# Softmax attention times a gated ReLU block: heads divided on VectorE between two 32x32 turns, and the transposes of the heads left out

## The chip, the cores and the metric

The kernel runs on one core of a Trainium2 chip. The metric is the device time of one execution in microseconds; the times given are medians of several runs. A core has five engines that run side by side, each with its own instruction queue: TensorE (PE in the profile, its weight loads PEld), VectorE (DVE), ScalarE (ACT), GpSimd (POOL) and SyncE (SP). SyncE only issues DMAs here; GpSimd issues some as well.

## The reference

```python
x = A_x                                   # 1 x 2048 x 576, fp32
xn = layernorm(x)                         # rows normalized, eps 1e-5
q, k, v = split(xn @ wqkv)                # 32 heads of 18 columns
p = softmax(q @ k.T * 18 ** -0.5)         # full, over 2048 keys
s = concat_heads(p @ v) @ wo
gate = xn @ W_gate; up = xn @ W_up        # 576 x 4608 each
g = silu((relu(gate) * up) @ W_down)
out = x + s * g
```

All products keep nearly fp32 precision: an operand is split into a high part (rounded to the fast fp32r type) and a low remainder, and three products (high x high, high x low, low x high) are summed in PSUM.

## The kernel before, in words

The work is one long stream of matmuls. A small planner in the source, `Lanes` (lines 30 to 211), keeps two lanes: the upper and the lower 64 rows of TensorE's array take different matmuls at the same time. The planner gives every part a PSUM bank out of eight, counts columns as time, keeps an estimate of when VectorE ("V") and ScalarE ("A") are free (`server`), and writes out the matmuls in the order it finds. `window` (line 169) takes a list of parts, a list of score matmuls to mix in, and inserts, which are called when a given share of the columns has been written out. A function `hold` (line 78) takes a bank for a step that uses all of the array, and `pause` advances both lanes. `keep` (line 262) pins an instruction to the program's order on its engine; what is not pinned may be moved by the scheduler that lowers the program. All matmuls and transposes are pinned, and so are some VectorE operations, but not the reductions at line 394. `load` (line 267) pins SyncE's DMAs until `in_order` is cleared at line 982.

**First stage** (lines 424 to 689). Tokens come in four groups `g` of 512. Rows are loaded (`load_rows`), their statistics taken on VectorE (`stats`, line 454), normalized on VectorE (`normalized_rows`, line 476; the first group half on ScalarE, `first_rows`), and transposed to features on TensorE (`turn`, line 499). Per group one window computes q and k (`pq`), evicted by ScalarE (high part, line 303) and VectorE (low part, line 304) into four buffers `hh` and stored to DRAM by GpSimd's queue (line 554); a second window computes v (`pv`). The steps of the next group's rows are inserts of the first window (`spread`, line 658). `spill` (line 532) stores the transposed rows to DRAM, five DMAs at once after the first window. GpSimd splits the weights (`split_pool`, line 307). Before the first useful product, `busy` (line 603) issues matmuls whose result is not used. GpSimd also clears the two value tiles `va` (lines 795 to 801), early in the program.

**Middle** (lines 966 to 1009). Two interleaved streams: the gated block runs over 144 units of 128 hidden columns (`pg`, `pu` for gate and up, `py` for down), two units to a `cycle` (line 934), and attention runs over 16 pairs of heads `u`, four cycles each. A cycle mixes in 32 score matmuls `pm` for the row maxima of the next pair, each reduced on VectorE (line 394, 128 rows to one column), and 32 score matmuls `psx`, whose exponentials ScalarE takes (line 880). After a cycle `attend` (line 896) multiplies eight key tiles with the values (`po`, 64 matmuls over four column groups of the array); the first of two sums is copied by ScalarE (line 914), the second added by VectorE (line 918). The exponentials need minus the row maximum, which rides in two extra rows of `qT`: `max_rows` (line 820) reduces, splits in high and low, transposes on TensorE (line 829, tile `tp`), copies out (line 833) and writes the rows with eight small DMAs (line 839). `finish_pair` (line 845) turns the sums `ot` (head columns x tokens) into rows with four transposes (line 862), divides by the sum of exponentials that came out as a column of the same product (lines 849 to 856), and stores rows to `od`. Both are put on the list `tasks` and run after `attend` of every second cycle (line 1008).

**End** (lines 1010 to 1118). The last two units and the last attention product are done, then `store_y` writes the last group's sums to DRAM. For each of 16 token tiles the heads are loaded as rows, turned by five transposes (`heads`, line 1050), split, and multiplied with `wo` in 28 matmuls (`pw`); `load_gate` (line 1031) loads the sums, ScalarE takes the sigmoid, GpSimd the product; VectorE multiplies (line 1111), GpSimd adds `x` (line 1115, for the last two tiles VectorE), and SyncE stores the output (line 1116). Tiles are taken in the order `horder`, the last gated group last.

Of the kernel before, what the change touches and what calls it, by code (L numbers as in the profile page):

```python
# [10 lines left out]
BF16 = mybir.dt.bfloat16  # L11
# [18 lines left out]
class Lanes:  # L30
# [4 lines left out]
    def __init__(self, banks, make, matmul, fence):  # L35
        self.make, self.matmul, self.fence = make, matmul, fence
        self.t = [0.0, 0.0]
        self.last = 0.0
        self.free = [0.0] * banks
        self.used = [False] * banks  # L40
        self.server = {"V": 0.0, "A": 0.0}
        self.main = [deque(), deque()]
        self.n = self.synced = self.fences = 0
        self.wrote = [0] * banks
        self.left = []
# [40 lines left out]
    def own(self, lane, name):  # L86
# [3 lines left out]
        return b, self.make(b, name)  # L90

# [48 lines left out]
    def part(self, p):  # L140
        by = min("AV", key=lambda e: self.server[e])
# [73 lines left out]
def kernel(  # L215
# [10 lines left out]
    nc = tc.nc  # L226
# [60 lines left out]
    od = dram.tile([S, D], F32, name="od")  # L287
# [70 lines left out]

    def strips(dst, src, u, cs, order):
# [22 lines left out]
    def maxima(u, h):  # L382
# [3 lines left out]
        def one(g, j, c):  # L386
            def fn():
# [5 lines left out]
                def reduce(ps):  # L393
                    nc.vector.tensor_reduce(mx[:, g % 2, h, j, c : c + 1], ps, axis=AX.X, op=ALU.max)  # L394
                    counts[u, g // 2] += 1
                    if counts[u, g // 2] == 4 * 4 * NQ:
                        tasks.append((max_rows, ([qTs[u, g - g % 2], qTs[u, g - g % 2 + 1]], mx)))
# [26 lines left out]
    with ExitStack() as st:  # L424
# [4 lines left out]
        def weights(name, n, outs, pl=one, first=None, **kw):  # L429
            gw = pl.tile([P, 2, KS, n], F32R, name=name, **kw)  # L430
            o = 0
            for cols in outs:
# [4 lines left out]
                if first is not None:  # L437
                    keep(nc.gpsimd.tensor_copy(hi, rg))
# [15 lines left out]
        def stats(xt, ln):  # L454
# [18 lines left out]
            ln += [xt, mv, rs]  # L473
            yield

        def normalized_rows(xt, mv, rs, xn):
            for j in range(4):
                nc.vector.tensor_scalar(
                    xn[:, j, :D], xt[:, j], mv[:, j, 0:1], rs[:, j : j + 1], op0=ALU.subtract, op1=ALU.mult
                )  # L480
                nc.vector.tensor_scalar(
                    xn[:, j, D:], xt[:, j, C4:], mv[:, j, 0:1], rs[:, j : j + 1], op0=ALU.subtract, op1=ALU.mult
                )
                if j % 2:
                    yield

        def first_rows(xt, mv, rs, xn):
            nb = one.tile([P, 4], F32, name="nb")
            nc.vector.scalar_tensor_tensor(nb, mv[:, :, 0], -1.0, rs, op0=ALU.mult, op1=ALU.mult)
            for j in range(2):  # L490
                nc.scalar.activation(
                    xn[:, 2 + j, :D], xt[:, 2 + j], AF.Identity, bias=nb[:, 2 + j : 3 + j], scale=rs[:, 2 + j : 3 + j]
                )
                nc.vector.tensor_scalar(
                    xn[:, j, :D], xt[:, j], mv[:, j, 0:1], rs[:, j : j + 1], op0=ALU.subtract, op1=ALU.mult
                )
# [35 lines left out]
        def spill(g):  # L532
            for c in range(KX):
                load(xTd[g, c], xs[g][c].rearrange("p a s -> p (a s)").bitcast(F32))
# [68 lines left out]
        def busy(xt):  # L603

            ones = one.tile([P, 512], F32R, name="ones")
            half = one.tile([P, 512], BF16, name="half")
# [3 lines left out]
            nc.gpsimd.memset(half, 1.0)  # L610
# [3 lines left out]
            ops = [(ones[:, :P], ones)] * 10 + [(xr[:, :P], xr[:, :512])] * 4  # L614
            ops += [(xr[:, :P], xr[:, 0:1].to_broadcast([P, 512]))] * 4
            ops += [(half[:, :P], half)] * 4 + [(ones[:, :P], ones)] * 4 + [(xr[:, 64:192], xr[:, 1:513])] * 4
            for l, r in ops:
                mm(ps, l, r, start=True, stop=True)
# [29 lines left out]
        def stepped(gen, at_):  # L648
            return [(w, lambda: next(gen, None)) for w in at_]

        for g in range(NQ):
# [6 lines left out]
            spread = [0.1 + 0.85 * i / 12 for i in range(12)]  # L658
# [3 lines left out]
            lanes.window(parts, None, ins)  # L662
            if g + 1 < NQ:
                spill(g)
# [22 lines left out]
            lanes.window([a + b for a, b in zip(va_, vb_)], scores)  # L687
# [57 lines left out]
    def add_up(j, n, f, side):  # L745
# [5 lines left out]
        def add(ps):  # L751
            nc.vector.tensor_tensor(ys[j][:, cs], ps[:, :HC], ys[j][:, cs], ALU.add)  # L752
# [42 lines left out]
    vas = []  # L795
    for i in range(2):
        va = two.tile([P, NT, VA + 32], F32, name=f"va{i}", bufs=1)
        nc.gpsimd.memset(va, 0.0)
        nc.gpsimd.memset(va[:, :, DH : DH + 1], 1.0)
        nc.gpsimd.memset(va[:, :, VA + DH : VA + DH + 1], 1.0)  # L800
        vas.append(va)
# [14 lines left out]
    def run_tasks(todo):  # L816
        for fn, args in todo:
            fn(*args)

    def max_rows(qs, mx):  # L820
# [3 lines left out]
        nc.vector.tensor_reduce(nm, mx, axis=AX.X, op=ALU.max, negate=True)  # L824
        nxr = nx.bitcast(F32R)
        nc.scalar.activation(nxr[:, :, :, 0], nm, AF.Copy)
        nc.vector.tensor_tensor(nxr[:, :, :, 1], nm, nx[:, :, :, 0], ALU.subtract)
        b, ps = lanes.hold("tp")
        tp(ps[0:32, 0:P], nx.rearrange("p q h a j -> p (q h a j)"), ident)
        nt_ = two.tile([32, P], F32, name="nt")  # L830

        def write(ps):
            nc.scalar.activation(nt_.bitcast(F32R), ps[0:32, 0:P], AF.Copy)
            for q, qT in enumerate(qs):
                for h in range(2):
                    for a in range(2):
                        r = h * R + KA + a
                        p0 = q * 16 + h * 8 + a * 4
                        nc.sync.dma_start(
                            qT[r : r + 1, :].rearrange("o (j t) -> o j t", t=P).bitcast(F32), nt_[p0 : p0 + 4, :]  # L840
                        )
# [303 lines left out]
```

## Time and profile before

| | |
|---|---|
| median of three runs | 2634.07 us (2632.28 to 2634.75) |
| the profiled execution, its own time | 2630.82 us |
| its span in the trace | 2629.0 us |
| granted TensorE clock, mean | 0.997 |
| TensorE busy, instructions | 2604.1 us, 25546 |
| VectorE busy, instructions | 1733.4 us, 2904 |
| ScalarE busy, instructions | 1465.8 us, 2780 |
| GpSimd busy, instructions | 1443.3 us, 1276 |

Rows of the profile give a group of instructions with its line in the source, its engine, the operation, the tiles written and read, shapes and count, then the busy time in us and the mean of one in ns, then idle time ahead of it and what ended it. A row of the chain gives start, length and the piece. A row of the windows gives the stretch, its length, then busy time and number of instructions of TensorE, its weight loads, VectorE, ScalarE and GpSimd, then the granted TensorE clock (1.00 is full), the DMA engines' busy share and GB/s. Matmul durations overlap, so the distance of starts is what passes. All times in traces are of the one profiled execution.

### The profile page before, as it was taken

How to read it: one execution, taken by the hardware profiler on the slowest of the kernel's cores; microseconds unless marked ns; L12 is line 12 of the kernel's file. 1: busy time of each engine (PE TensorE's matmuls, PEld its weight loads, DVE VectorE, ACT ScalarE, POOL GpSimd, SP SyncE). 2: the span in 40 equal slices, each digit the busy share in tenths (PEclk: the TensorE clock that was granted, in tenths of full speed). 3: DMA queues.
4: the chain of work that ended last, by engine and by line, in shares of the span. 5: the costliest groups of instructions: out<-in, count | busy, mean ns of one | idle time of the engine just before them, and what ended most of it. 6: DMA issues, size and time to landing. Idle time of an engine off the chain costs nothing.

```text
span 2629.0 us, 63025 instructions
## 1 busy us (share of the span) xinstructions
PE 2604.1 (99%) x25546; PEld 2122.5 (81%) x25546; DVE 1733.4 (66%) x2904; ACT 1465.8 (56%) x2780; POOL 1443.3 (55%) x1276
## 2 busy tenths in 40 slices
PE   7999999999999999999999999999999999999999
PEld 6999888777788887777777777788877777777789
DVE  5326557777777777777777777777777777776124
ACT  2221136666666666666666666666666666666662
POOL 5236785555555555555555555555555555555555
PEclk8999999999999999999999999999999999999999
DMA  7644332222332222222242222222232222222247
GB/s 245 211 155 143 88 102 68 76 69 72 100 95 65 75 69 73 69 69 74 73 132 69 76 66 66 73 67 75 72 109 82 67 76 71 73 66 58 58 125 236
DMA packets 293267, 243.72 MB, mean 93 GB/s; under 512 B 64496, under 2 KB 236272, under 8 KB 292976
## 3 DMA queue, kind: packets, MB, share of 16 engines
q1 hardware_dynamic: 286192, 216.08, 28.3%
q0 software_dynamic: 6784, 23.60, 2.7%
q8 instruction: 202, 3.31, 0.5%
q14 instruction: 89, 0.73, 0.1%
HBM read 193.45 MB, written 45.61 MB: 91 GB/s over the span
## 4 chain that ended last, share of the span: by engine, by line
PE 93%; DMA 2%; POOL 1%; DVE 1%; SPq 1%; ACT 1%; issue 0%; ACTq 0%; POOLq 0%; DVEq 0%
PE pg L272 23%; PE po L272 17%; PE py L272 16%; PE pu L272 10%; PE psx L272 10%; PE pm L272 9%; PE pq L272 4%; PE pv L272 2%; PE pw L272 1%; PE tp L275 1%; DMA gt<-yd 0%; DMA qd<-hh 0%; DMA out_dram<-xr 0%; DMA rd<-in_B_W_down_dram 0%; PE tps L275 0%
## 5 line engine op out<-in xcount | busy, mean ns | idle before, releaser
L394 DVE TENSOR_REDUCE mx<-pm 128x1 f32<-128x512 f32 x2048 | 1379.4, 689 | 245.1 <-PE pm L272 163.3
L880 ACT ACTIVATE p<-psx 128x512 f32<-128x512 f32 x2048 | 1181.7, 598 | 542.3 <-PE pm L272 254.4
L272 PE MATMUL pg<-x,gw 64*128 64x512 f32 x3888 | 1157.2, 392 | 3.2 <-POOL gw L309 2.3
L272 PE MATMUL pu<-x,gw 64*128 64x512 f32 x3888 | 1144.2, 392 | 0.0
L272 PE MATMUL pm<-kT,qT 54*128 54x512 f32 x2048 | 793.5, 397 | 0.0
L272 PE MATMUL psx<-qT,kT 56*128 56x512 f32 x2048 | 786.0, 394 | 0.0
L272 PEld LDWEIGHTS pg<-x,gw 64*128 64x128 f32 x3888 | 719.3, 186 | 61.3 <-POOL gw L309 3.2
L272 PEld LDWEIGHTS pu<-x,gw 64*128 64x128 f32 x3888 | 717.3, 187 | 22.9
L272 PE MATMUL py<-dw,hh 64*128 64x288 f32 x6864 | 717.2, 295 | 2.1 <-POOL dw L309 0.9
L272 PEld LDWEIGHTS py<-dw,hh 64*128 64x128 f32 x6864 | 662.0, 186 | 51.6 <-issue 31.1
L272 PE MATMUL po<-p,va 128*32 128x512 f32 x4096 | 452.7, 594 | 0.4 <-ACT p L880 0.4
L730 POOL CAST hh<-h 128x512 fp32r<-128x512 f32 x127 | 77.6, 611 | 611.6 <-DVE h L727 611.6
L757 POOL TENSOR_TENSOR y<-yt,y 128x288 f32<-128x288 f32 x268 | 215.1, 806 | 325.4 <-ACT yt L756 325.3
L272 PEld LDWEIGHTS psx<-qT,kT 56*128 56x128 f32 x2048 | 375.2, 185 | 19.9
L309 POOL TENSOR_TENSOR gw<-rg,gw 128x1152 fp32r<-128x1152 f32 x144 | 383.6, 2664 | 11.6
L272 PEld LDWEIGHTS pm<-kT,qT 54*128 54x128 f32 x2048 | 371.5, 185 | 13.3
L272 PEld LDWEIGHTS po<-p,va 128*32 128x32 f32 x4096 | 126.4, 110 | 279.0 <-issue 269.0
L309 POOL TENSOR_TENSOR dw<-rd,dw 128x576 fp32r<-128x576 f32 x144 | 205.0, 1423 | 11.5
L733 POOL TENSOR_TENSOR hh<-h,hh 128x512 fp32r<-128x512 f32 x144 | 186.3, 1294 | 36.0 <-ACT hh L732 25.7
L308 POOL CAST gw<-rg 128x1152 fp32r<-128x1152 f32 x144 | 165.3, 1148 | 23.5 <-DMA qT<-qd 9.0
L752 DVE TENSOR_TENSOR y<-py,y 128x288 f32<-128x288 f32 x268 | 120.4, 449 | 50.1 <-PE py L272 49.7
L723 ACT ACTIVATE h<-pg 128x512 f32<-128x512 f32 x144 | 85.9, 596 | 112.3 <-PE pg L272 76.9
(96 smaller groups left out, 1379.4 us busy)
## 6 DMA issues: line engine op xcount, KB each, us to landing
rd<-in_B_W_down_dram SPq DMA_DIRECT2D x144, 288.0 KB
rg<-in_B_W_gate_dram SPq DMA_DIRECT2D x144, 256.0 KB
rg<-in_B_W_up_dram SPq DMA_DIRECT2D x144, 256.0 KB
qT<-qd SPq DMA_DIRECT2D x384, 36.0 KB
kT<-kd SPq DMA_DIRECT2D x384, 36.0 KB
kd<-hh POOLq DMA_DIRECT2D x16, 512.0 KB, 5.4
qd<-hh POOLq DMA_DIRECT2D x16, 512.0 KB, 6.0
xTd<-x SPq DMA_DIRECT2D x15, 512.0 KB
```

The lines of the kernel that those rows point to most:

```text
L272: return keep(nc.tensor.matmul(*args, **kw))
L275: return keep(nc.tensor.transpose(*args))
L308: keep(nc.gpsimd.tensor_copy(hi, raw))
L309: keep(nc.gpsimd.tensor_tensor(lo, raw, hi.bitcast(F32), ALU.subtract))
L394: nc.vector.tensor_reduce(mx[:, g % 2, h, j, c : c + 1], ps, axis=AX.X, op=ALU.max)
L723: nc.scalar.activation(made[0], ps, AF.Relu)
L730: keep(nc.gpsimd.tensor_copy(hh[:, 0], h))
L733: keep(nc.gpsimd.tensor_tensor(hh[:, 1], h, hh[:, 0].bitcast(F32), ALU.subtract))
L752: nc.vector.tensor_tensor(ys[j][:, cs], ps[:, :HC], ys[j][:, cs], ALU.add)
L757: keep(nc.gpsimd.tensor_tensor(ys[j][:, cs], t, ys[j][:, cs], ALU.add))
L880: nc.scalar.activation(p[0][:, h, i, :], ps, AF.Exp, scale=SCALE)
```

## The change

- Every VectorE operation of the middle is pinned to program order (`keep`).
- `max_rows` is a generator now: the tile of maxima is turned in 32x32 blocks by VectorE, stored to a small DRAM tile `nd` and loaded from there into the rows of `qT`; its steps are run behind a cycle and as inserts of the next one.
- `divide` takes the place of `finish_pair`: VectorE turns the sums in 32x32 blocks, divides, turns them back, and stores heads as features; `od` is features x tokens now. It runs behind the cycle after its `attend`.
- At the end heads are loaded as features, without transposes; the last group's sums stay in the chip; VectorE adds `x` for all tiles; GpSimd's queue stores the output.
- At the start ScalarE normalizes rows (VectorE three of the first four), ScalarE makes the high part of the first weight, the inserts begin earlier, `spill` is spread over the second window, the fences of the second window lie on VectorE alone, `busy` uses other operands, and the value tiles are cleared in the middle stage's first cycles.

```diff
-    od = dram.tile([S, D], F32, name="od")
+    od = dram.tile([D, S], F32, name="od")
+    nd = dram.tile([2, 32, P], F32, name="nd")
...
-        by = min("AV", key=lambda e: self.server[e])
+        by = min(self.by, key=lambda e: self.server[e])
...
+    def works(self, server, length):
+        self.server[server] = max(self.server[server], min(self.t)) + length
...
-                    nc.vector.tensor_reduce(mx[:, g % 2, h, j, c : c + 1], ps, axis=AX.X, op=ALU.max)
+                    keep(nc.vector.tensor_reduce(mx[:, g % 2, h, j, c : c + 1], ps, axis=AX.X, op=ALU.max))
...
-                    keep(nc.gpsimd.tensor_copy(hi, rg))
+                    nc.scalar.activation(hi, rg, AF.Copy)
...
+        def normalized_rows(xt, mv, rs, nb, xn):
+            for j in range(4):
+                by_scalar(xt, nb, rs, xn, j)
+                yield
+            nc.scalar.activation(xn[:, :, D:], xn[:, :, C4:D], AF.Copy)
+
+        def by_scalar(xt, nb, rs, xn, j):
+            nc.scalar.activation(
+                xn[:, j, :D], xt[:, j], AF.Identity, bias=nb[:, j : j + 1], scale=rs[:, j : j + 1]
+            )
...
-            spread = [0.1 + 0.85 * i / 12 for i in range(12)]
+            spread = [0.04 + 0.9 * i / 15 for i in range(14)]
...
+            ins = []
             if g + 1 < NQ:
-                spill(g)
+                ins = [(0.05 + 0.15 * c, lambda c=c: spill(g, c)) for c in range(KX)]
...
+            lanes.by = "V" if g < NQ - 1 else "AV"
+            lanes.window([a + b for a, b in zip(va_, vb_)], scores, ins)
+            lanes.by = "AV"
...
-        b, ps = lanes.hold("tp")
-        tp(ps[0:32, 0:P], nx.rearrange("p q h a j -> p (q h a j)"), ident)
-        nt_ = two.tile([32, P], F32, name="nt")
...
+        lanes.works("V", 0.3)
+        lanes.works("A", 0.25)
+        yield
+        keep(nc.vector.tensor_tensor(nxr[:, :, :, 1], nm, nx[:, :, :, 0], ALU.subtract))
+        nt_ = two.tile([P, 32], F32, name="nt")
+        keep(nc.vector.transpose(nt_, nx.rearrange("p q h a j -> p (q h a j)")))
+        lanes.works("V", 0.7)
+        n_ = nd[rows_kept[0] % 2]
+        rows_kept[0] += 1
+        load(n_.rearrange("c (b t) -> b c t", b=4), nt_)
+        yield
+        for q, qT in enumerate(qs):
+            for h in range(2):
+                r, p0 = h * R + KA, q * 16 + h * 8
+                load(qT[r : r + 2, :].bitcast(F32), n_[p0 : p0 + 8, :].rearrange("(a j) t -> a (j t)", a=2))
+        yield
+
+    def divide(u, qp, ot):
+
+        oT = two.tile([P, 512], F32, name="oT", bufs=1)
+        o3 = oT.rearrange("p (k d) -> p k d", d=32)
+        rc = two.tile([P, 16], F32, name="rc")
+        keep(nc.vector.transpose(oT, ot))
+        lanes.works("V", 0.75)
+        yield
+        keep(nc.vector.reciprocal(rc, o3[:, :, DH]))
+        by = rc.unsqueeze(2).to_broadcast([P, 16, DH])
+        keep(nc.vector.tensor_tensor(o3[:, :, :DH], o3[:, :, :DH], by, ALU.mult))
+        lanes.works("V", 0.9)
+        yield
+        keep(nc.vector.transpose(ot, oT))
+        lanes.works("V", 0.75)
+        for h in range(2):
+            for i in range(2):
+                s_ = 32 * (2 * h + i)
+                f0, t0 = (2 * u + h) * DH, (2 * qp + i) * 512
+                nc.sync.dma_start(od[f0 : f0 + DH, t0 : t0 + 512], ot[s_ : s_ + DH, :])
+        yield
...
+        for gen in rows:
+            ins += stepped(gen, (0.3, 0.5, 0.8))
...
+        if i == 3:
+            clear_v()
...
+            cycle(N1 + UN * u + 2 * i, scores, (), rows)
+            rows = now
+            for gen in [*later, *now]:
+                for _ in range(4 if gen in later else 2):
+                    next(gen, None)
+            later.clear()
...
-            attend(u, qp, done)
-            run_tasks(now)
-            del tasks[: len(now)]
+            attend(u, qp)
...
+        o = fo.tile([P, 5, P], F32, name="o")
+        ks = slice(k * P, (k + 1) * P)
+        nc.sync.dma_start(o[:, :4], od[:C4, ks].rearrange("(c p) t -> p c t", p=P))
+        for d in range(2):
+            nc.sync.dma_start(o[d * DT : (d + 1) * DT, 4], od[C4:, ks])
...
-        ps = any_bank("tps")
-        for c in range(4):
-            tp(ps[:, c * P : (c + 1) * P], o[:, c * P : (c + 1) * P], ident)
+        o4 = o.rearrange("p c t -> p (c t)")[:, :512]
...
-            if i + 2 >= NT:
-                nc.vector.tensor_tensor(xt[:, cs], xt[:, cs], gt[:, cs], ALU.add)
-        if i + 2 < NT:
-            nc.gpsimd.tensor_tensor(xt, xt, gt, ALU.add)
-        nc.sync.dma_start(out2[k * P : (k + 1) * P, :], xt)
+            nc.vector.tensor_tensor(xt[:, cs], xt[:, cs], gt[:, cs], ALU.add)
+        nc.gpsimd.dma_start(out2[k * P : (k + 1) * P, :], xt)
```

167 lines of the change are left out of this document (61 added, 106 removed).

## The prediction

> **What bounds the kernel now.** I read the page first (busy shares, the chain that ended last by engine), then the long pieces of the chain of waits, then the timeline around them, and last the table by windows.
>
> ```profile
> span 2629.0 us, 63025 instructions
> PE 2604.1 (99%) x25546; PEld 2122.5 (81%) x25546; DVE 1733.4 (66%) x2904; ACT 1465.8 (56%) x2780; POOL 1443.3 (55%) x1276
> PE 93%; DMA 2%; POOL 1%; DVE 1%; SPq 1%; ACT 1%; issue 0%; ACTq 0%; POOLq 0%; DVEq 0%
> ```
>
> TensorE is busy for 99% of the span, and 93% of the chain is TensorE. So what leaves TensorE in the middle comes off the time, if no other engine is late in its place; what is moved between other engines counts only where TensorE waits, at the two ends of the span.
>
> Next the chain's long pieces. Three successive attention blocks (po) from the middle; with a fixed number of matmuls between them, their distances show what one kind of stretch has more than the other:
>
> ```profile
> 1088.34 7.00 PE po L272 x64
> 1122.77 7.00 PE po L272 x64
> 1156.56 3.55 PE po L272 x29
> ```
>
> The first distance is 34.43 us, the second 33.79 us. The timeline behind the first and behind the second block shows why (start, length, engine, line, operation):
>
> ```profile
> 1095.28 0.28 PE L275 MATMUL tp<-ident,nx 128*32 128x128 f32 x1
> 1095.40 0.60 PE L275 MATMUL tp<-ident,ot 128*128 128x128 f32 x4
> 1095.93 0.93 PE L272 MATMUL py<-dw,hh 64*128 64x288 f32 x10
> ```
> ```profile
> 1129.70 0.94 PE L272 MATMUL py<-dw,hh 64*128 64x288 f32 x10
> ```
>
> In the first case five transposes stand between po and the next py, and po start to py start is 7.59 us; in the second nothing stands there and it is 6.93 us.
>
> **The change part by part.**
>
> *A, the middle.* Removed from TensorE: the five transposes of every second stretch. Price: 34.43 - 33.79 = 0.64 us. The count comes from the group of the tp transposes:
>
> ```profile
> L275 PE MATMUL tp<-ident,ot 128*128 128x128 f32 x128 | 19.3, 273 | 0.0
> ```
>
> 128 in fours are 32 pairs of blocks; the last pair lies in the end stage (B). So 31 x 0.64 = 19.8 us. The same row shows a second way to price them, 273 ns each, which would be 128 x 0.273 = 35 us; but four take 0.60 us from first start to last end, since they overlap, and the distance of the blocks is what the span pays. The Trainium skill, page "TensorE: Matmul & The Clock Gate", section "Part 4: PE-mode transpose", gives about 275 ns for one in a kernel; by it part A would be 35 us and the whole sum some 15 us larger. The trace agrees with that as a duration (273) and not as a price (0.64 for five).
>
> Added to VectorE in the same place: two turns of 128x512, a reciprocal, one multiply of 128x288, one turn of 128x32. Removed: a reciprocal and two multiplies of 128x144. The work sits in program order after the last reduction of a stretch and before po's sum, so under po:
>
> ```profile
> 1122.70:1129.70 7.00, 7.00 (x66) 1.98 (x64) 1.83 (x5) 0.81 (x3) 6.84 (x6) 1.00 0.27 81
> 1129.70:1156.50 26.80, 26.80 (x273) 25.30 (x270) 23.58 (x37) 20.14 (x37) 11.69 (x12) 1.00 0.24 70
> L394 DVE TENSOR_REDUCE mx<-pm 128x1 f32<-128x512 f32 x2048 | 1379.4, 689 | 245.1 <-PE pm L272 163.3 <-PE psx L272 31.3 <-PE pg L272 11.0
> L309 POOL TENSOR_TENSOR gw<-rg,gw 128x1152 fp32r<-128x1152 f32 x144 | 383.6, 2664 | 11.6
> ```
>
> The number after TensorE's and its weight loads' is VectorE's: 1.83 us busy in the 7.00 us of po, so 5.17 us free. No row shows a 32x32 turn. Lower bound: a 128x512 reduction, 0.69 us. Upper bound: the same, behind a whole long subtraction of GpSimd each time, 0.69 + 2.66 = 3.35 us. I take 0.7, since the 2048 reductions beside the same GpSimd work average 689 ns. Then two turns 1.4, the small turn 0.2, reciprocal and multiply under 0.8: 2.4 us, plus one wait of at most 2.66 us when the multiply meets GpSimd's long subtraction, 5.1 of 5.17. What spills over finds 3.2 us (26.80 - 23.58) in the next stretch. I cost it at nothing, at the upper bound it is rival 2. The fixed order of VectorE's instructions costs nothing in the same way: TensorE issues in program order and VectorE follows it.
>
> On SyncE's queue the eight small row DMAs of a max pair become one store and four loads, the one store of heads becomes four; ten issues for nine, nothing in the middle.
>
> *B, the end.* The transposes of the last pair and of three tiles stand ahead of the first output product, five more between the products of each two tiles:
>
> ```profile
> 2555.02 0.60 PE L275 MATMUL tp<-ident,ot 128*128 128x128 f32 x4
> 2557.01 2.04 PE L272 MATMUL pw<-wo,hf 128*128 128x288 f32 x12
> ```
> ```profile
> 2561.73 3.71 PE pw L272 x28
> 2565.43 0.55 PE tps L275 x5
> 2565.98 3.71 PE pw L272 x28
> ```
> ```profile
> 2561.73:2612.78 51.05, 51.04 (x397) 50.80 (x396) 19.59 (x44) 15.62 (x34) 32.42 (x23) 1.00 0.85 268
> ```
>
> The first removal is 1.99 us (2557.01 - 2555.02). A tile takes 4.25 us (2565.98 - 2561.73), 3.71 without its transposes, and 13 of them follow. But three things come close to 3.71. VectorE has 19.59 us in 12 tiles, 1.63 a tile, and gets the two additions that GpSimd had:
>
> ```profile
> 2621.19 1.43 POOL L1115 TENSOR_TENSOR xr<-xr,gt 128x576 f32<-128x576 f32 x1 [0.91 <-DVE gt L1111]
> 2621.51 1.43 DVE L1113 TENSOR_TENSOR xr<-xr,gt 128x288 f32<-128x288 f32 x1
> 2625.05 0.46 DVE L1113 TENSOR_TENSOR xr<-xr,gt 128x288 f32<-128x288 f32 x1
> ```
>
> Alone an addition takes 0.46, beside GpSimd 1.43. So VectorE has 1.63 + 0.92 = 2.55 us, and up to 3.98 if it loses a whole GpSimd operation a tile (only the gate's product is left there). The DMA engines were busy 85% of the 51.05, 3.6 us a tile, and the heads now come in rows of 512 bytes instead of 2304; the last four tiles load no gate. I take 3.9 us a tile between 3.71 and 4.25: 13 x 0.35 = 4.6 us. The last output leaves by GpSimd's queue: from the end of the last addition (2625.51) to the span's end is 3.5 us now, and GpSimd's own stores take 5.4 us to land
>
> ```profile
> kd<-hh POOLq DMA_DIRECT2D x16, 512.0 KB, 5.4
> ```
>
> so 0 to 1.9 more; I take 1.0. B = 2.0 + 4.6 - 1.0 = 5.6 us; ends 0.1 and 9.0.
>
> *C, the start.* The windows, and the chain through them:
>
> ```profile
> 33.20:40.00 6.80, 1.32 (x12) 0.85 (x10) 6.80 (x8) 0.17 (x1) 6.64 (x6) 0.89 0.46 105
> 40.00:46.00 6.00, 6.00 (x38) 5.25 (x38) 2.21 (x6) 1.15 (x4) 1.03 (x2) 0.56 0.96 351
> 58.50:61.80 3.30, 0.01 (x2) 0.01 (x2) 0.69 (x1) 0.83 (x2) 0.72 (x1) 1.00 1.02 415
> 61.80:66.00 4.20, 4.20 (x40) 4.20 (x42) 0.69 (x1) 0.78 (x2) 0.72 (x1) 0.59 1.03 400
> ```
> ```profile
> 31.99 0.58 DVE xn L478
> 36.98 1.91 DVE xn L481
> 39.65 0.80 DVE hh L304 x2
> 45.35 1.15 POOL wqk L308
> 49.92 11.54 DMA qd<-hh
> ```
>
> TensorE stands for 5.48 us (6.80 - 1.32) and 3.29 us, and after each it runs at a granted clock of 0.56 and 0.59, which costs 6.00 x 0.44 = 2.6 and 4.20 x 0.41 = 1.7: 13.1 us in all. The first hole is the normalizing of the next rows: from 31.99 to 39.65 VectorE stretches eight operations whose alone-time is 0.58 and less, because GpSimd splits weights beside it. ScalarE, busy 0.17 of that window, takes these over. What is late next is the store of q and k: its DMA lands 11.54 us after 49.92, behind GpSimd's split of a weight that comes at 45.35, with the DMA engines at 1.0. That part moves forward only as far as VectorE's hh at 39.65 moves forward, and the bytes stay. Ends 0 and 13.1; I take 6.
>
> *D, the first half-filled stretches.* A hole at the first max rows:
>
> ```profile
> 269.84 5.06 SPq L839 DMA_DIRECT2D qT<-nt  x8
> 277.26 0.52 SPq L268 DMA_DIRECT2D rd<-in_B_W_down_dram  x1
> ```
> ```profile
> 260.00:300.00 40.00, 36.73 (x361) 31.57 (x359) 16.62 (x30) 6.29 (x14) 27.44 (x24) 0.96 0.25 72
> ```
> ```profile
> L798 POOL MEMSET va<- 128x832 f32 x2 | 1.5, 785 | 0.0
> ```
>
> Eight issues hold SyncE for 5.06 us, the weights behind them come late, TensorE stands 3.27 us and loses 0.04 x 40 = 1.6 at the lower clock: 4.9. The changed kernel issues fewer, one stretch apart. Against it, GpSimd clears the value tiles here (1.5 us) instead of ahead of all work. I take 2.5, ends -1.5 and 4.9.
>
> **Sum.** 19.8 + 5.6 + 6 + 2.5 = 33.9 us. The profiled execution took 2630.8 us, so it would take 2596.9; the median of the runs, 2634.1, stands 3.3 us above it and goes to 2600.2.
>
> **The rivals.** 1. *Only the middle pays.* The q and k stores keep their landing time, so C is 0; VectorE is the end's bound at 3.98 us a tile, so B is 2.0 + 13 x 0.27 - 1.9 = 3.6; D is 0. Then 23.4 us, 2610.7. For it speaks the DMA share of 1.02 to 1.03 at 58 to 66 us and the 1.43 us row; against it that GpSimd has one operation left a tile and VectorE finds 0.9 us of additions only. Chance 0.22. The Trainium skill, page "SBUF — State Buffer", section "Who interferes with whom", states that a VectorE operation with two SBUF inputs and a GpSimd operation that reads SBUF exclude each other for the whole instruction; it speaks against moving the additions. By that rule the 3.98 holds at every tile; the trace agrees in the pair at 2621.
>
> 2. *VectorE's turns queue behind GpSimd and become the bound.* Under po GpSimd is busy 6.84 of 7.00 us. If each of the two big turns waits a whole long subtraction, as the multiply may, VectorE needs 2 x 3.35 + 1.0 + 2.66 = 10.4 us; 5.17 lie under po and 3.2 in the next stretch, where its fixed order puts the reductions, and the PSUM banks that they free, behind them. It decides from 33.9 / 31 = 1.1 us a pair that finds no cover; at 10.4 us it is 2.0, so 31 x 2.0 - 33.9 = 28 us slower, 2662. For it: the 6.84 of 7.00, and the addition of 0.46 that took 1.43. Against it: the reductions' 689 ns show VectorE operations with one input that GpSimd does not stretch. Chance 0.05.
>
> 3. *The transposes were not what the distance shows*, and the planner's order of banks gives the 0.64 back by waits of the same size, with only C and D left: 2634.1 - 8.5 = 2625.6. Against it: TensorE has no idle time in the windows of the middle. Chance 0.05.
>
> **How the numbers follow.** My forecast, 2600 us, has 0.68; the rivals 0.22, 0.05 and 0.05. Its own range, by the bounds of B, C and D, runs from 2634.1 - 46.8 = 2587 to 2634.1 - 18.4 = 2616, and holds rival 1 too; the runs before lie 2.5 us apart, which I add at both ends: 2584 to 2618. What is left out are rivals 2 and 3 and the outermost of the bounds. A difference within 0.2% (5.3 us) can't be told from none: of rival 3's 0.05 I count 0.03 as same, since with C at its lower end only 2.5 us are left. Faster 0.68 + 0.22 + 0.02 = 0.92, same 0.03, slower 0.05.
>
> **What would show it.** Distances of po of 33.8 us throughout: A right. Turns of about 0.7 us that lie under po, no wait of TensorE for VectorE. Tiles of the end 3.7 to 4.0 us apart. No hole at 33 us and at 277 us; a hole that only moves to the q and k stores is rival 1. Wrong would be: new waits of py, pm or pg on VectorE; a hole behind the clearing of the value tiles; an end that waits for DMA as long as before.

## The result, and the profile after

The changed kernel takes 2611.15 us, median of its runs (2609.53 to 2611.91), beside 2634.41 us for the kernel before on the same chip (2632.28 to 2636.52). The ratio is 0.9911, 95% interval 0.9894 to 0.9928: 23.3 us faster. The forecast was 33.9 us, so 10.6 us are missing. The profiled execution took 2609.53 us with a span of 2607.8. The rest of this section divides the difference of the two spans, 21.2 us (2629.0 - 2607.8); the medians differ by 2.1 more, as the two profiled executions lie 3.6 and 1.6 us below their medians.

The page:

```profile
span 2607.8 us, 62736 instructions
PE 2575.4 (99%) x25308; PEld 2106.7 (81%) x25308; DVE 1785.9 (68%) x2976; ACT 1471.0 (56%) x2763; POOL 1440.5 (55%) x1276
```

TensorE's busy time fell by 28.7 us, which is more than the span did: some of what left TensorE came back as standing time. Six times in both traces say where, five of them when TensorE begins (or ends) the piece named:

| | before | after | gained up to here | gained in this part |
|---|---|---|---|---|
| pv resumes in the first stretch | 61.79 | 61.68 | 0.1 | C: 0.1 |
| first po | 406.99 | 403.96 | 3.0 | D: 2.9 |
| last po | 2541.56 | 2518.64 | 22.9 | A: 19.9 |
| first pw | 2557.01 | 2536.74 | 20.3 | B, entry: -2.6 |
| last pw ends | 2624.17 | 2597.89 | 26.3 | B, tiles: 6.0 |
| span ends | 2629.0 | 2607.8 | 21.2 | B, tail: -5.1 |

A and D are what was forecast (19.8 and 2.5). C was forecast at 6 and is nothing. B was forecast at 5.6 and is -1.7.

The middle, in the chain of waits: three successive attention blocks.

```profile
1079.54 7.00 PE po L275 x64
1113.35 7.00 PE po L275 x64
1147.13 7.00 PE po L275 x64
```

Both distances are 33.8 us now; the 34.43 is gone. VectorE's new work, in the groups by line (busy time, mean of one):

```profile
L861 DVE STREAM_TRANSPOSE oT<-ot 128x512 f32<-128x512 f32 x32 | 22.4, 700 | 0.0
L869 DVE STREAM_TRANSPOSE ot<-oT 128x512 f32<-128x512 f32 x32 | 22.8, 711 | 1.1
L866 DVE TENSOR_TENSOR oT<-oT,rc 128x288 f32<-128x288 f32 x32 | 16.2, 507 | 1.1
L844 DVE STREAM_TRANSPOSE nt<-nx 128x32 f32<-128x32 f32 x32 | 6.8, 212 | 1.1
```

The start, by windows: TensorE's hole at 33 us, where it waited for VectorE, has shrunk from 5.5 to 0.5 us (6.80 - 6.28); the one before 61.8 us is still there.

```profile
33.20:40.00 6.80, 6.28 (x50) 5.04 (x52) 3.81 (x8) 4.49 (x11) 6.17 (x5) 0.75 0.44 112
58.50:61.80 3.30, 0.12 (x2) 0.12 (x2) 0.62 (x2) 0.60 (x1) 0.72 (x1) 0.50 1.00 358
61.80:66.00 4.20, 4.20 (x38) 4.20 (x40) 0.31 (x1) 0.71 (x2) 0.72 (x1) 0.55 1.03 416
```

What TensorE waited for in all, from the table of waits (total, times, longest), shows that it grew to 9.0 us, and that a wait at the end is new:

```profile
PE pv L275 <- DVEq L298: 9.0, 1, 9.0
PE py L275 <- DVE ot L929: 3.1, 1, 3.1
```

And the chain that leads to the 9.0 us:

```profile
40.28 4.79 DMA rgw<-in_A_wqkv_dram
45.12 1.15 POOL wqk L312
46.35 2.67 POOL wqk L313
49.02 0.64 POOL kd L558
49.66 11.03 DMA qd<-hh
60.79 0.61 ACT hh L307
61.68 4.37 PE pv L275 x35
```

It is the chain of before, within 0.3 us up to the start of the store. ScalarE's seventh and eighth hh tiles need buffers whose stores have not landed; GpSimd issues these stores behind the split of wqk4 (lines 312 and 313), and that split waits for its weights, which land at 45.06 us.

### The profile page after: what moved, and what is told of

Same layout as the page of the kernel before. It is cut to its first block, busy times and chain, and to the rows that moved or that the text cites. A ratio compares the mean times of both kernels' runs of the same rounds, so it can differ in the third digit from the quotient of the medians.

```text
span 2607.8 us, 62736 instructions
## 1 busy us (share of the span) xinstructions
PE 2575.4 (99%) x25308; PEld 2106.7 (81%) x25308; DVE 1785.9 (68%) x2976; ACT 1471.0 (56%) x2763; POOL 1440.5 (55%) x1276
## 4 chain that ended last, share of the span: by engine, by line
PE 92%; DMA 3%; POOL 2%; DVE 1%; SPq 1%; issue 1%; ACT 0%; POOLq 0%; DVEq 0%; ACTq 0%
PE pg L275 19%; PE po L275 17%; PE py L275 16%; PE pu L275 15%; PE pm L275 10%; PE psx L275 9%; PE pq L275 3%; PE pv L275 2%; SPq L271 1%; PE pw L275 1%; DMA rgw<-in_A_wqkv_dram 0%; DMA qd<-hh 0%; DMA gt<-yd 0%; DMA rg<-in_B_W_up_dram 0%; DMA kT<-kd 0%
## 5 line engine op out<-in xcount | busy, mean ns | idle before, releaser
L313 POOL TENSOR_TENSOR dw<-rd,dw 128x576 fp32r<-128x576 f32 x144 | 212.2, 1474 | 11.5
L929 DVE TENSOR_TENSOR ot<-po,ot 128x512 f32<-128x512 f32 x32 | 22.1, 691 | 188.4 <-PE po L275 188.4
```

Source lines behind the costliest of these rows:

```text
L313: keep(nc.gpsimd.tensor_tensor(lo, raw, hi.bitcast(F32), ALU.subtract))
L929: keep(nc.vector.tensor_tensor(ot, ps, ot, ALU.add))
```

## The experiments

All twelve ran beside the kernel before; ratios are against it. Shifts of a few us are read from the starts in the traces, since the intervals of two ratios can't part them. One caution: in seven profiles with the same start as the changed kernel's (this one and six below) pv resumes between 59.6 and 63.1 us, so shifts of a start of that kind count from some 3.5 us on; the distance from there to the first po repeats within 1.2 us (341.1 to 342.3 in six of them).

**1. The load and split of wqk4 later** (two kernels: load and split, and the split alone).

```diff
-        wqk.append(weights("wqk4", P, ...))
         for i in range(3):
             turn(0, xn0, i)
...
             lanes.window(parts, None, ins)
+            if g == 0:
+                wqk.append(weights("wqk4", P, ...))
```

> The load and the split of the fifth block of query/key weights (wqk4) are issued after the first stretch of columns instead of ahead of it; nothing else differs from the changed kernel. In the changed kernel TensorE stands 9.0 us before 61.68 us, because ScalarE's seventh hh tile waits for a store of an earlier one, and GpSimd issues that store behind the wqk4 split, whose weights land at 45.06 us. Theory (order in GpSimd's queue): stores 3 and 4 leave about 10 us earlier, the 9.0 us hole shrinks to 0 to 3 us, the first po matmul comes at 395 to 398 us instead of 404.0, and the run takes some 6 to 9 us less than the changed kernel (about 2603 us). Rival (the DMA engines, share of time 1.0 from 46 to 62 us, set the landing): the stores land hardly sooner; as one load less lies ahead of them the hole loses 2 to 4 us at most, first po at 400 to 402 us.

> As the run before it, but the load of wqk4 stays where it was and only GpSimd's split of it is issued after the first stretch of columns. Theory (order in GpSimd's queue): the same gain as with the load moved too, first po at 395 to 398 us, some 6 to 9 us less than the changed kernel. Rival (DMA engines full): the load still goes ahead of the stores, so the hole keeps 7 to 9 us and first po stays within 1.5 us of 404.0.

Measured: 2598.73 us, ratio 0.9869 (0.9855 to 0.9884), and 2599.86 us, 0.9870 (0.9855 to 0.9885). First po at 391.25 and 391.87 us, 12.7 and 12.1 us earlier and more than the theory's 395 to 398. The window from 46 to 66 us in the changed kernel, with both moved, and with the split alone moved:

```profile
46.00:66.00 20.00, 11.01 (x117) 10.44 (x115) 2.07 (x3) 2.51 (x5) 7.20 (x8) 0.74 1.02 395
```
```profile
46.00:66.00 20.00, 19.80 (x260) 18.55 (x259) 5.03 (x12) 4.53 (x11) 9.58 (x9) 1.00 1.03 393
```
```profile
46.00:66.00 20.00, 20.00 (x263) 19.67 (x261) 4.02 (x10) 4.66 (x11) 10.31 (x10) 1.00 1.03 385
```

TensorE works through it at full clock (1.00 for 0.74), while the DMA engines' share and rate are the same. With the split moved alone GpSimd issues the fourth store at 40.45 us instead of 49.66, although the load stays ahead of it. So the rival, full DMA engines, falls, and the order of GpSimd's queue is shown as the cause. The gain is larger than the 9.0 us of the hole, since the low clock behind it goes too: 0.45 x 4.20 = 1.9 us by the last window of the section above. The 1.2 to 1.8 us that remain lie within the scatter of a start.

**2. The same edit in the kernel before.**

> The kernel before the change with one edit: load and split of wqk4 are issued behind the first stretch of columns. In the kernel before, TensorE stands twice at the start: 5.5 us at 33 us for VectorE's normalizing, and 3.4 us at 58 us for a chain of stores that resumes at 61.79 us, as it does in the changed kernel (61.68 us). Theory (two chains in parallel: the stores' chain ended last and hid what the normalizing by ScalarE saves): with the stores' chain away the normalizing's hole stays, so the first po comes at 399 to 402 us instead of 407.0, and the kernel gains 5 to 8 us where the changed one gained 12; the difference of 5 to 6 us is what ScalarE's normalizing is worth once it is not hidden. Rival (the normalizing was never worth anything, because the hole at 33 us is made up before the stretch ends): the same gain of about 12 us as in the changed kernel, first po at 394 to 395 us.

Measured: 2628.46 us, ratio 0.9977 (0.9968 to 0.9987); first po at 402.22 us, 4.8 us earlier than before. The old hole is all that is left (waits of TensorE from 25 to 75 us, and two windows):

```profile
PE tps L275 <- DVE xn L478: 5.7, 4, 2.2
PE pv L272 <- ACTq L294: 0.4, 1, 0.4
```
```profile
33.20:40.00 6.80, 1.39 (x10) 0.96 (x12) 6.80 (x9) 0.07 (x1) 6.49 (x5) 0.83 0.45 106
40.00:46.00 6.00, 6.00 (x43) 5.25 (x43) 2.31 (x6) 1.25 (x4) 1.45 (x2) 0.62 1.04 399
```

By the medians it gains 5.5 us; the first po comes 0.2 us behind the theory's 399 to 402. The theory holds: two chains ran side by side, and each edit alone is worth little (the changes of the start, normalizing by ScalarE among them, 0.1 us up to pv; the split later 4.8 us), both together, with D, 15.7 us (406.99 - 391.25).

**3. The normalizing back on VectorE, wqk4 later.** From the first kernel of experiment 1, with the operations of `normalized_rows` back on VectorE.

```diff
-                by_scalar(xt, nb, rs, xn, j)
+                nc.vector.tensor_scalar(xn[:, j, :D], xt[:, j], mv[:, j, 0:1], ...)
+                nc.vector.tensor_scalar(xn[:, j, D:], xt[:, j, C4:], mv[:, j, 0:1], ...)
                 yield
-            nc.scalar.activation(xn[:, :, D:], xn[:, :, C4:D], AF.Copy)
```

> The changed kernel with wqk4 behind the first stretch (first po at 391.3 us, 2599 us), and in it the normalizing of the rows of the second and later stretches put back on VectorE; the rest of the change stays. Theory (with the stores' chain away the normalizing is late next): TensorE stands about 5.5 us at 33 us and then runs at a clock of about 0.6 for 6 us, so first po comes 7 to 9 us later, at 398 to 400 us, and the run takes 2606 to 2608 us. Rival (the difference of 11.0 us between the first po of the two kernels with wqk4 later comes from the max rows and the planner's order, not from the normalizing): first po stays below 394 us.

Measured: 2603.78 us, ratio 0.9881 (0.9867 to 0.9894); first po at 396.35 us.

```profile
33.20:40.00 6.80, 3.70 (x17) 2.45 (x18) 6.80 (x7) 0.66 (x2) 5.76 (x4) 0.63 0.42 95
```

Both expectations missed: 396.35 lies between 398 to 400 and below 394. TensorE stands 3.1 us of this window, not 5.4; the other edits of the start (earlier inserts, the first rows and the first weight) stay in this run, but which of them makes the difference is not shown. So the normalizing is worth 5.1 us where it is not hidden, and D and those other edits share the remaining 5.9 of the 11.0 us between 402.22 and 391.25.

**4. TensorE's transposes back.**

```diff
+    def turned():
...
+        b, ps = lanes.hold("tp2")
+        for j in range(4):
+            tp(ps[:, j * P : (j + 1) * P], ident, ident)
+        tp(ps[:32, :P], ident[:, :32], ident)
+        lanes.evict(b, ps, lanes.pause(0.6), [("V", 0.1, ...)])
...
             attend(u, qp)
+            if i % 2 == 0 and u + i:
+                turned()
```

> To the changed kernel five transposes on TensorE are added back behind every second attention block (31 times; they turn the identity matrix into a bank that only a one-column copy reads, so nothing depends on them); VectorE's turns stay. Theory (the middle's gain is TensorE's time, 0.64 us a pair): the distances of po alternate 33.8 and 34.4 us again, the stretch from the first to the last po grows by 31 x 0.64 = 19.8 us, and the run takes about 2631 us. Rival (the gain of the middle came from the planner's order of banks, not from the transposes themselves): the distances stay at 33.8, or grow at other places, and the run grows by less than 8 us.

Measured: 2629.5 us, ratio 0.9985 (0.9976 to 0.9993), 18.4 us above the changed kernel. Attention blocks in the chain:

```profile
438.18 7.00 PE po L275 x64
471.95 7.00 PE po L275 x64
506.41 7.00 PE po L275 x64
540.17 7.00 PE po L275 x64
```

Distances of 33.77, 34.46, 33.76 us. From the first to the last po it takes 2134.97 us, in the changed kernel 2114.68: 20.3 us, 0.65 for five transposes. A is shown from both sides. The added piece takes a bank from the planner as well; but TensorE has no idle time in the middle (busy 1995.70 of the 1995.70 us from 404.3 us on), so what it adds is TensorE's time and no wait for a bank. The prediction weighed as a price the duration that the Trainium skill gives for one transpose, about 275 ns (page "TensorE: Matmul & The Clock Gate", section "Part 4: PE-mode transpose"). In this trace one takes 287 ns (128x128) or 273 ns (the small one), and 124 and 31 of them would be 44 us; the run pays 20.3, so it too bears the figure out as a duration and not as a price.

**5. VectorE's turns doubled, and five times.** `nc.vector.transpose(oT, ot)` and its counterpart are repeated in place.

> Each of VectorE's two 128x512 turns is issued twice, which gives the same values; nothing else differs from the changed kernel. This adds 2 x 0.7 = 1.4 us of VectorE to every pair of attention blocks, 45 us in all. Theory (the turns lie under po's 7 us, where VectorE was idle for 5.17 us): the distances of po stay at 33.8 us and the time within 4 us of the changed kernel's 2611. Rival (VectorE is close to the bound there, or its turns queue behind GpSimd): a part of the 1.4 us shows at every second distance of po; from 0.3 us a pair on it is 9 us or more, all of it would be 43 us.

> Each of VectorE's two 128x512 turns is issued five times, which gives the same values; nothing else differs from the changed kernel. This adds 8 x 0.71 = 5.7 us of VectorE to every pair of attention blocks. In the changed kernel VectorE is busy for 3.6 us of the po that the turns lie under and idle for 3.4; in the stretch behind it is idle for 3.8 of 26.8. Theory (slack in the next stretch also covers): 3.4 us go under po, the other 2.3 into the next stretch, and a pair grows by 0.3 us at most, the run by less than 10 us. Rival (VectorE's fixed order puts the reductions behind the turns, and TensorE waits for the banks that they free): what goes beyond po shows in full, 2.3 us a pair, 31 x 2.3 = 71 us, about 2680 us.

Measured: doubled 2609.31 us, ratio 0.9905 (0.9892 to 0.9919), and 2114.71 us from first to last po beside 2114.68: nothing. Five times: 2708.19 us, ratio 1.0281 (1.0267 to 1.0295), and 2212.28 us: 97.6 us more, 3.1 us a pair. VectorE in one pair of that run (start, length):

```profile
1104.94 3.69 DVE L862 STREAM_TRANSPOSE oT<-ot 128x512 f32<-128x512 f32 x5
1108.95 2.63 DVE L867 TENSOR_TENSOR oT<-oT,rc 128x288 f32<-128x288 f32 x1
1111.62 3.69 DVE L871 STREAM_TRANSPOSE ot<-oT 128x512 f32<-128x512 f32 x5
```

The turns keep 0.71 us each (mean of 160). The multiply between them, 2.63 us here, takes 1.54 on the mean, in the changed kernel 0.51; so VectorE has 6.7 us more in a pair. The theory that the next stretch's idle time covers the rest falls. TensorE's waits from the first to the last po are two (total, times, longest):

```profile
PE psx L275 <- ACT p L893: 45.8, 29, 2.6
PE pm L275 <- DVE mx L401: 6.3, 15, 0.4
```

The rival's path, reductions that come late and the banks that they free, is the second and smaller one. The first runs over ScalarE: its small step of the max rows (`nx`) needs VectorE's `nm`, which stands behind the turns, and the exponentials stand behind `nx`. In the pair shown:

```profile
1115.24 0.17 DVE L836 TENSOR_REDUCE nm<-mx 128x16 f32<-128x64 f32 x1
1115.44 0.21 ACT L838 ACTIVATE nx<-nm 128x16 fp32r<-128x16 f32 x1 [3.82 <-DVE nm L836]
1116.20 0.79 PE L275 MATMUL psx<-qT,kT 56*128 56x512 f32 x1 [2.60 <-ACT p L893]
```

The first reduction behind the turns starts at 1116.04 us, so the rival's wait lies close behind. The waits are 52.1 of the 97.6 us; the other 45 are the same 20790 matmuls taking longer (TensorE busy 2159.3 us for 2114.3). Behind the wait of this pair the clock was 0.50 and then 0.55 from 1116.2 to 1123 us. The rival's 71 us lie between the waits and the whole and match neither.

**6. The max rows at once, as before the change.**

```diff
-        now = tasks[:]
+        cycle(k, [...], loads)
+        for gen in tasks:
+            for _ in gen:
+                pass
         tasks.clear()
-        cycle(k, [...], loads, now)
```

> In the changed kernel, the steps for the max rows of the first, half-filled stretches are all issued right behind the stretch in which the last maximum was taken, as before the change, instead of within the following stretch; the turn on VectorE, the one store and the four loads stay as they are. The first 62 us are the same program, so the shift of the first po against the first resumption of pv (404.00 - 61.68 = 342.3 us in the changed kernel, 407.02 - 61.79 = 345.2 before) is what counts. Theory (the 2.9 us come from issuing the rows one stretch later, since SyncE stands for them ahead of the weights' loads): the distance goes back to 344.5 to 347 us, TensorE again stands 2 to 5 us near 280 us. Rival (they come from five DMA issues in place of eight): the distance stays below 343.3 us.

Measured: 2611.21 us, ratio 0.9915 (0.9902 to 0.9929). First po at 405.33, pv resumed at 60.99: 344.3 us, between the changed kernel's 342.3 and 345.2 before. The window near 280 us loses its clock again (this run first, then the changed kernel):

```profile
260.00:300.00 40.00, 37.37 (x368) 31.69 (x365) 17.62 (x33) 6.15 (x13) 28.10 (x28) 0.96 0.27 75
260.00:300.00 40.00, 37.53 (x384) 32.50 (x382) 19.75 (x36) 6.04 (x13) 30.04 (x30) 1.00 0.29 85
```

TensorE stands 2.6 us of it here and 2.5 in the changed kernel, where its longest wait there is 1.3 us instead of 2.0. So the later issue saves the low clock (0.04 x 40 = 1.6 us) and hardly the standing time. The distance of 344.3 misses the theory's 344.5 by 0.2 and is well above the rival's 343.3. By the changed kernel's own distance 2.0 of D's 2.9 us are the later issue, by the other five up to 3.2; whether the smaller number of DMAs has a part is not settled.

**7. The end: bank order, and buffers.** First the banks alone (`po_bank` is set in `attend` to the bank of the last po), then the rows' buffers alone.

```diff
+    turns[0] = po_bank[0]
```
```diff
-        xt = f2.tile([P, D], F32, name="xr")
+        xt = f2.tile([P, D], F32, name="xr", bufs=8)
```

> The banks of the last stage are taken in turn from the one behind that of the last attention's po, so that the first py no longer lands in po's bank; nothing else differs from the changed kernel. In the changed kernel TensorE stands 3.06 us before the first py at 2528.78 us, whose releaser is VectorE's ot addition, the reader of that bank, itself behind VectorE's two hf subtractions (2.99 us). Theory (bank order costs the entry of the end): the 3.06 us go, the 48 py matmuls take 6.6 us instead of 8.1, and the first pw comes 17.0 to 18.5 us after the start of the last po instead of 18.10; with clock and wait gone some 3 to 4.5 us less, so 13.5 to 15.5 us is what the theory asks for. Rival (VectorE is late anyway at this place): the wait moves to the py tiles' own additions or to the first pw, which still starts 17.5 to 18.5 us after the last po, and the time is within 1 us of the changed kernel's.

> The tile of x rows of the last stage has 8 buffers instead of 4; nothing else differs from the changed kernel. In the changed kernel 10 us lie between TensorE's last matmul and the end of the span (4.8 before the change), and the loads of the last x rows wait 26.8 us for output stores to land. Theory (a buffer whose output store must land holds up the last rows): with 8 buffers the last additions no longer wait 1.75 us for x rows, and the tail comes down to 5 to 6 us, 4 to 5 us less in all. Rival (VectorE and GpSimd slow each other and GpSimd's gates stand ahead of its stores): the loads come early, but the tail keeps 8.5 to 10 us and the time stays within 1.5 us of the changed kernel's.

Banks: 2609.86 us, ratio 0.9909 (0.9893 to 0.9926), no gain. But TensorE's timeline shows that the wait is gone:

```profile
2519.44 7.07 PE L275 MATMUL po<-p,va 128*32 128x512 f32 x64 [0.41 <-ACT p L891]
2526.44 6.63 PE L275 MATMUL py<-dw,hh 128*128 128x288 f32 x48
2532.91 1.74 PE L275 MATMUL pw<-wo,hf 128*128 128x288 f32 x12
```

From the last po to the first pw it is 13.47 us (18.10 in the changed kernel, 15.45 before): the entry that was forecast. The 16 tiles, from first to last pw, then take 67.3 us instead of 61.2 and give it all back. SyncE's waits and ScalarE's in this run name the taker:

```profile
SPq L1055 <- DMA out_dram<-xr: 28.3, 11, 5.5
ACT hf L1067 <- DMA o<-od: 20.7, 10, 5.0
```

SyncE loads rows, heads and gates in one queue. The load of a row waits for a buffer whose output has not landed, and the loads of heads behind it wait too. Buffers: 2606.07 us, ratio 0.9892 (0.9877 to 0.9907). SyncE no longer waits at that line, the tiles take 59.6 us, and from the last pw to the end it is 6.5 us instead of 9.9. The theory asked for a tail of 5 to 6 us and 4 to 5 less in all; it is 0.5 longer, and 5.1 us less in all.

**8. Three mends together** (wqk4 later, banks, buffers), **and with the last three stores on SyncE.**

```diff
-        nc.gpsimd.dma_start(out2[k * P : (k + 1) * P, :], xt)
+        (nc.gpsimd if i + 3 < NT else nc.sync).dma_start(out2[k * P : (k + 1) * P, :], xt)
```

> The changed kernel with three edits together: load and split of wqk4 behind the first stretch, banks of the last stage from the one behind po's, 8 buffers of x rows. Theory (each of the three took away a wait of its own): the start gives 12.7 us by the first po, the entry of the end 4.6 us (18.1 to 13.5 us from the last po to the first pw), and with the rows' loads no longer in front of the heads' loads on SyncE's queue the last tiles take 59.3 us and the tail 6.6, 5 us together: about 2589 us. Rival (the DMA engines, share 0.92 to 0.97 in the tiles of the run with 8 buffers, are the end's bound, so that an earlier entry only makes TensorE wait for heads): the entry's 4.6 us come back inside the tiles, 2594 us.

> The kernel with the three mends, and the output stores of the last three tiles issued by SyncE instead of GpSimd. With the mends 5.3 us lie between the end of VectorE's last addition (2583.66 us) and the end of the span (2589.0); before the change, with SyncE's stores, 3.5. Theory (GpSimd's stores are issued later and land later): 3.3 to 3.8 us from the last addition to the end, 1.5 to 2 us less in all, about 2588 us. Rival (the landing time is that of the traffic, whichever engine issues): 5 to 5.5 us again, and the same time.

Three mends: 2589.94 us, ratio 0.9833 (0.9819 to 0.9846). The chain of the end:

```profile
2508.57 7.07 PE po L275 x64
2515.64 6.56 PE py L275 x48
2522.20 27.84 PE pw L275 x210
```

The entry keeps its 4.6 us and the tiles stay at 59.6, as the theory had it; the rival's 2594 us do not come. Banks and buffers were two waits in a row, and the first pays only when the second is gone. Stores on SyncE: 2588.66 us, ratio 0.9826 (0.9813 to 0.9839). From the end of VectorE's last addition to the end of the span it is 3.5 us; with GpSimd's stores it is 5.3 (after, and with the three mends), before 3.5. The whole gains less, since in this run one tile waited 1.1 us for VectorE; the two intervals do not part these two versions.

## Why the prediction was right or wrong

**A, right.** 19.8 forecast, 19.9 measured. The price by distances, 0.64 us for five, held in both directions (4). VectorE's turns at 0.7 and 0.2 us were right too (0.70, 0.71 and 0.21), and so was their cover: doubled they cost nothing, and of 6.7 us more in a pair 1.7 showed as waits (52.1 / 31), so that some 5 us were free, an estimate from experiment 5. Rival 2, turns that queue behind GpSimd, did not come: the turns are not stretched, and the multiply, for which alone the prediction allowed it, hardly (458 ns in the median, 1077 at most, 507 on the mean). Rival 3 falls: the middle has no idle time in the changed kernel either (busy 1996.00 of the 1996.00 us from 404 us on), and experiment 4 brings the longer distances back.

**D, right in size.** 2.5 forecast, 2.9 measured, of which at least 2.0 by the later issue (6); the smaller number of DMAs was not tested alone. Its sign, no hole at 277 us, did not come in full: TensorE still stands 2.5 us between 260 and 300 us, before 3.3. What went is mainly the low clock.

**C, wrong: 0.1 for 6** (a start scatters by up to 3.5 us). The step that failed: "That part moves forward only as far as VectorE's hh at 39.65 moves forward, and the bytes stay." The hh was earlier: VectorE's third and fourth tiles end at 37.4 us, before at 40.8. GpSimd issued their stores only 0.3 us earlier (48.94 and 49.66 us, before 49.20 and 49.92). Between the rows at 39.65 and 45.35 us that the prediction quotes, the chain of before has one more, which ties it to VectorE there:

```profile
40.45 4.90 DMA xTd<-x
```

But the split of 45.35 us reads the loaded weights (rgw) and not xTd. SyncE issued the last part of their load at 39.8 us before the change and at 40.3 us after it, and in the changed kernel the profile names that load as what the split waited for. So the chain was read as hanging on VectorE, where it hung on GpSimd's queue and on a load; that the load held the split in the kernel before too is inferred from these times. Rival 1 had this zero ("The q and k stores keep their landing time"), but for the DMA share of 1.02, and that reason is wrong: with the order mended the share stays at 1.03 and the hole is gone (1). Its sign, a hole that only moves to the stores, came: TensorE's wait there is 3.4 us before and 9.0 after. The 5.48 us of the first hole were hidden by the other chain: the normalizing is worth 5.1 us where nothing covers it (3).

**B, wrong: -1.7 for 5.6.** The mechanism of the entry and of the tiles was right and two waits were missed.

- Entry: 2.0 forecast, -2.6 measured. The end takes its banks in turn, from the same first one in both kernels. In the changed kernel the planner's order has put the last po into that bank; in the kernel before, and in experiment 4, py shows no such wait. So the first py stands until VectorE has read po for ot, behind two hf subtractions (VectorE's timeline; po ends at 2525.7):

```profile
2525.04 2.99 DVE L1067 TENSOR_TENSOR hf<-o,hf 128x512 fp32r<-128x512 f32 x2 [6.29 <-ACT hf L1066]
2527.95 0.68 DVE L929 TENSOR_TENSOR ot<-po,ot 128x512 f32<-128x512 f32 x1
```

  The wait is 3.1 us, and the 48 py matmuls behind it take 8.1 us instead of 6.6, at a clock of 0.79: 2.0 - 3.1 - 1.5 = -2.6. A new wait of py for VectorE is one of the signs by which the prediction said that it would be wrong. With the bank moved the forecast 2.0 come out (15.45 - 13.47).
- Tiles: 4.6 forecast, 6.0 measured. The 16 tiles take 3.82 us each on the mean (61.2 / 16), with eight buffers 3.72, so VectorE and DMA did not hold them at the 3.9 that was feared. Two tiles' first matmuls in TensorE's timeline are 3.71 us apart, all that TensorE needs:

```profile
2553.43 1.76 PE L275 MATMUL pw<-wo,hf 128*128 128x288 f32 x12
2557.14 1.76 PE L275 MATMUL pw<-wo,hf 128*128 128x288 f32 x12
```

- Tail: -1.0 forecast, -5.1 measured. The landing of GpSimd's store costs 1.8 us (5.3 - 3.5), within the 0 to 1.9 given. The other 3.3 are rows that come late: SyncE held three loads of rows at

```profile
2589.54 8.78 SPq L1054 DMA_DIRECT2D xr<-in_A_x_dram  x3
```

since the four buffers come free only when a store has landed. SyncE's waits for that are 20.6 us in all before the change and 26.8 after it, and with eight buffers the 3.3 us are gone (7). One reason is in GpSimd's queue: behind three gates it issues a store 1.2 us after the addition (2585.86 and 2587.08 us). How much of the 3.3 us that is, no run shows, since none moves all the stores back.

The sum of rival 1, 2610.7, came within 0.5 us of the result, for other reasons in B: no 3.98 us a tile, but a bank, and a buffer. That is luck, and so in part is that the forecast's wide range, 2584 to 2618, holds the result: of its four terms A and D were right, B and C were not.

## What to carry to other kernels

A hole belongs to the chain that ends last, and a chain that the edit does not touch keeps its landing time: before a moved step is credited with a stall, look for what stands ahead of its DMA in the queue that issues it, and for a load that this queue waits for. When work between two uses of a buffer or a bank is taken out, ask which buffer, bank or queue slot is now asked for earlier than it comes free; such waits stand in a row, so an edit that brings nothing alone may pay when the next wait is gone too.

## What the runs showed of the hardware

- A DMA share of 1.03 at 393 GB/s was no bound: TensorE worked through it at full clock once the order in a queue was right, and stood 9.0 us beside a share of 1.02 at 395 GB/s when it was not.
- VectorE's subtraction for the heads' low part grew longer when its first input came from SBUF instead of PSUM, with the same shape and GpSimd at work in both. Its groups before and after:

```profile
L1057 DVE TENSOR_TENSOR hf<-tps,hf 128x512 fp32r<-128x512 f32 x16 | 11.0, 689 | 16.8 <-ACT hf L1056 16.7
```
```profile
L1067 DVE TENSOR_TENSOR hf<-o,hf 128x512 fp32r<-128x512 f32 x16 | 17.8, 1122 | 11.9 <-ACT hf L1066 11.8
```

  The Trainium skill, page "SBUF — State Buffer", section "Who interferes with whom", states it so: VectorE contends with GpSimd's reads when both of its inputs lie in SBUF, not with one. The trace agrees, 1122 for 689 ns on the mean; the prediction had used the rule for the additions and missed it for the subtractions, which the change moves from one side of it to the other.
- The 32x32 turn of 128x512 took 0.70 to 0.71 us on the mean in every run. In the pair of experiment 5 GpSimd subtracts beside both groups of turns (1.42 and 1.44 us), and the mean of 160 stays at 0.71, while the multiply there, with two inputs in SBUF, took 2.63.
- With a last output store by GpSimd the span ended 5.3 us behind VectorE's last addition, in each of eleven profiles, with one by SyncE 3.5 to 3.6 us, in three. The Trainium skill, page "DMA: Bandwidth & Descriptors", section "Issuing engine by pattern", calls DMAs issued by SyncE or ScalarE generally faster than those of GpSimd; the traces agree, by 1.8 us here.
